# Hedgehog attention and a maxout layer on one core: q and k transposed in blocks of two tokens, q projected by 64-row pairs, its maximum applied as a factor on one of two numerator sums

## The chip, the cores and the metric

The kernel runs on one core of one Trainium2 chip. The metric is the device time of one execution in microseconds (us). The engines are called by their names or by the profile's short ones: TensorE (PE, its weight loads PEld), VectorE (DVE), ScalarE (ACT), GpSimd (POOL), and SyncE (SP), which issues transfers.

## The reference

Inputs q, k, v have 8 batches x 8 heads x 576 tokens x 64; `w_phi` is 64 x 128. The attention result is laid out as 4608 tokens x 512 and goes through a maxout layer of three 512 x 768 matrices and one 768 x 512 matrix.

```python
def phi(x):
    proj = x @ w_phi                                   # 64 -> 128
    proj = proj - max(abs(proj), axis=-1, keepdims=True)
    return concatenate([exp(proj), exp(-proj)], axis=-1)   # as in the reference: the max is subtracted once, then +/-

q_p, k_p = phi(q), phi(k)
kv  = einsum('bhsf,bhsd->bhfd', k_p, v)
z   = sum(k_p, axis=tokens)
num = einsum('bhsf,bhfd->bhsd', q_p, kv)
den = einsum('bhsf,bhf->bhs', q_p, z)[..., None] + 1e-06
x   = num / den                                        # 4608 x 512
h   = maximum(maximum(x @ w1, x @ w2), x @ w3)
out = h @ w_out
```

With m the maximum of |proj| of a token, the first half of the features is exp(proj - m), and the second, exp(-(proj - m)), is exp(-proj + m).

## The kernel before, in words

**Units.** The attention is done in 16 units; a unit is four heads of one batch, taken as two pairs `pr`, each of two heads `ab`. A pair's tokens lie on the partitions (64 per head, two heads above each other) in 9 columns, so a unit has 18 tiles of 128 tokens by 64 features. Units 0 to 3 (`BY_PE`) have q and k transposed by TensorE, units 4 to 15 by a transposing transfer on SP's queue. Unit 0 loads q and k on SP in float32 and casts them on VectorE and ScalarE, units 1 to 3 load them with a casting transfer on POOL's queue, units 4 to 15 load float32 and cast on POOL (line 474).

**Steps of a unit, by the node kinds of the code.**
- `T`, `Tc`: the transposition and its copy to `qkT`. Before, `qkT` holds q on partitions 0 to 63 and k on 64 to 127 of the same 128 columns.
- `G` (line 531): projections with the tokens as outputs, 64 rows each, q and k as a pair on the two row halves; five groups of 4, 4, 4, 4 and 2 tiles, each into two PSUM banks, `psq` and `psk`. ScalarE writes exp(+/-proj) of k to `Ek` (line 544), VectorE takes the maxima of |proj| of q and k (line 550) into `mqp` and `mk`.
- `R`, `mT`, `V` (units 2 to 15): the maxima of q are transposed by TensorE (line 558), copied to SBUF (line 562) and written by a transfer (line 566) into row 64 of `qkT`, in the place of a row of k that is no longer needed.
- `M` (lines 610 to 615): the projection of q with the features as outputs, in five products. The stationary matrix `wphi_m` has -1 in row 64, so the maximum is subtracted by the product itself. In units 0 and 1 it is subtracted by small extra products with `minus` (line 615). ScalarE writes exp(+/-) of it to `Eq` (line 623).
- `E`, `va`, `vd`: exp(-m) and exp(+m) of k (`em`), multiplied into v on POOL (line 585).
- `K` (line 639): 72 products into `kvps`; `kv`: their copies.
- `N` (line 657): ten products for one head of a pair, a numerator *block*; the two halves of the features are added in PSUM, in one bank `psn` of 5 x 65. Four blocks in a unit.
- `x` (lines 663, 664): the reciprocal of column 65 and the quotient, on VectorE.
- `X`: the transposition of the result to `xT`, by TensorE with a copy `Xc` in units 0 and 1, by a transfer on SP after that.

**The maxout layer** runs in nine chunks of 512 tokens: eight of one batch each, once its two units are done, and a last one from the ninth columns of all batches. max(x w1, x w2, x w3) is taken as x w1 plus a maximum of differences: 12 `up` steps of four 512-wide products each (line 710) with the `w_bf` differences (line 781), evictions `t1` on ScalarE or VectorE (lines 718, 720) and `h` on VectorE (line 716), then four `down` steps (lines 738, 743), their copies `osb` (line 751) and stores (line 758).

**What sets the order.** A table written out in the source, `PLAN`, gives every node its engine, its place in the order and its buffers. `plan` sorts the nodes by the table and each engine runs its share in this order; nothing is decided at run time but the waits on semaphores. All PSUM tiles share eight banks, and the table names the bank. `fill` puts products on constants (`idler`) into TensorE's planned gaps.

## Time and profile before

| | |
|---|---|
| time of the kernel, median of 3 runs | 283.17 us (282.54 to 283.33) |
| span of the profiled execution, first to last instruction | 281.1 us |
| what lies around the span, median less span | 2.1 us |
| PE busy | 273.2 us, 97% |
| DVE busy | 201.2 us, 72% |
| ACT busy | 197.0 us, 70% |
| POOL busy | 126.6 us, 45% |

The profile doesn't give a time of its execution besides the span, so the profiled execution's own time is taken as the span and 2.1 us around it. Busy time of TensorE counts a product from its start to its modelled end; neighbouring products overlap, so the distance from one start to the next is the better price. The shares are means over the head, the attention stretch (to about 235 us) and the maxout layer's end, which have different limits; they are to be read by stretch.

### The profile page before, as it was taken

How to read it: one execution, taken by the hardware profiler on the slowest of the kernel's cores; microseconds unless marked ns; L12 is line 12 of the kernel's file. 1: busy time of each engine (PE TensorE's matmuls, PEld its weight loads, DVE VectorE, ACT ScalarE, POOL GpSimd, SP SyncE). 2: the span in 40 equal slices, each digit the busy share in tenths (PEclk: the TensorE clock that was granted, in tenths of full speed). 3: DMA queues.
4: the chain of work that ended last, by engine and by line, in shares of the span. 5: the costliest groups of instructions: out<-in, count | busy, mean ns of one | idle time of the engine just before them, and what ended most of it. 6: DMA issues, size and time to landing. Idle time of an engine off the chain costs nothing.

```text
span 281.1 us, 8518 instructions
## 1 busy us (share of the span) xinstructions
PE 273.2 (97%) x3542; PEld 153.6 (55%) x3542; DVE 201.2 (72%) x426; ACT 197.0 (70%) x455; POOL 126.6 (45%) x112
## 2 busy tenths in 40 slices
PE   8889999999999999998999999999999999999995
PEld 3567665565565565565455556554544655444442
DVE  3999899998799797976798769875565383225342
ACT  3899889997889997876877998787737590321111
POOL 5489999847734634855528481410601500000000
PEclk9999999999999999999999999999999999999999
DMA  7999998999999989799997987976021035331065
GB/s 230 210 212 259 322 215 245 289 269 204 253 204 341 152 158 357 174 264 234 257 232 228 323 187 160 219 152 178 3 47 40 3 77 94 75 77 37 8 141 188
DMA packets 67552, 51.43 MB, mean 183 GB/s; under 512 B 48762, under 2 KB 52922, under 8 KB 67514
## 3 DMA queue, kind: packets, MB, share of 16 engines
q1 hardware_dynamic: 62084, 42.21, 62.1%
q0 software_dynamic: 4720, 7.87, 12.8%
q10 hardware_dynamic: 710, 0.83, 0.8%
q8 instruction: 27, 0.44, 0.6%
q14 instruction: 11, 0.09, 0.1%
HBM read 34.64 MB, written 9.44 MB: 157 GB/s over the span
## 4 chain that ended last, share of the span: by engine, by line
PE 81%; POOL 7%; DMA 6%; DVE 3%; issue 1%; ACT 1%; POOLq 0%
PE ups L710 30%; PE ops L743 15%; PE ops L738 11%; PE psn L657 6%; PE kvps L639 6%; PE psq L531 4%; PE psm L610 4%; DMA q_raw<-in_q_dram 3%; POOL vab L585 2%; DMA qk_bf<-in_k_dram 2%; POOL w_bf L781 2%; POOL qk_bf L474 2%; DVE mqp L550 1%; PE pm L807 1%; DVE mk L550 1%
## 5 line engine op out<-in xcount | busy, mean ns | idle before, releaser
L585 POOL TENSOR_TENSOR vab<-v_raw,em 128x1152 bf16<-128x1152 f32 (+1 forms) x36 | 68.2, 1908 | 83.9 <-ACT em L581 39.5
L710 PE MATMUL ups<-xT,w_bf 128*128 128x512 bf16 x432 | 102.4, 379 | 0.1
L544 ACT ACTIVATE Ek<-psk 128x512 bf16<-128x512 f32 (+1 forms) x156 | 81.5, 575 | 11.9 <-PE psk L531 9.3
L623 ACT ACTIVATE Eq<-psm 128x512 bf16<-128x512 f32 (+1 forms) x160 | 80.4, 584 | 3.5 <-PE psm L610 2.8
L710 PEld LDWEIGHTS <-w_bf 128*128 128x128 bf16 x432 | 40.7, 98 | 45.1 <-DVE x_sb L664 0.2
L550 DVE TENSOR_REDUCE mqp<-psq 128x4 bf16<-128x512 f32 (+1 forms) x80 | 48.5, 632 | 9.8 <-PE psk L531 9.7
L550 DVE TENSOR_REDUCE mk<-psk 128x4 f32<-128x512 f32 (+1 forms) x78 | 48.4, 635 | 4.3 <-PE psk L531 2.3
L743 PE MATMUL ops<-wout_bf,hT 128*128 128x512 bf16 (+2 forms) x222 | 51.1, 373 | 0.0
L716 DVE TENSOR_TENSOR hT<-hT,ups 128x512 bf16<-128x512 bf16 x54 | 35.6, 681 | 19.8 <-PE ups L710 18.7
L751 ACT COPY osb<-ops 128x512 f32<-128x512 f32 x25 | 14.6, 589 | 33.2 <-PE ops L743 24.1
L664 DVE TENSOR_TENSOR x_sb<-psn,rden 128x320 bf16<-128x320 f32 x64 | 31.5, 492 | 2.2
L743 PEld LDWEIGHTS <-hT 128*128 128x128 bf16 x222 | 20.5, 98 | 22.0
L718 ACT ACTIVATE hT<-ups 128x512 bf16<-128x512 f32 x32 | 18.8, 616 | 18.2 <-PE ups L710 18.1
L657 PEld LDWEIGHTS <-Eq 128*128 128x128 bf16 x640 | 25.7, 97 | 9.5 <-issue 0.6
L657 PE MATMUL psn<-kv_sb,Eq 128*128 128x65 bf16 x640 | 27.4, 193 | 0.1
L738 PE MATMUL ops<-xT 128*128 128x512 bf16 x96 | 24.2, 379 | 0.0
L720 DVE TENSOR_SCALAR hT<-ups 128x512 bf16<-128x512 f32 x22 | 15.0, 686 | 12.5 <-PE ups L710 12.5
L531 PE MATMUL psq<-w,qkT 64*128 64x128 bf16 x284 | 23.3, 217 | 0.4 <-DVE qkT L494 0.2
L531 PE MATMUL psk<-w,qkT 64*128 64x128 bf16 x284 | 23.1, 217 | 0.0
L639 PE MATMUL kvps<-vab,Ek 64*128 64x65 bf16 x1152 | 20.6, 190 | 2.5 <-POOL vab L595 1.0
L531 PEld LDWEIGHTS <-qkT 64*128 64x128 bf16 x568 | 16.4, 94 | 10.1 <-issue 7.9
L610 PE MATMUL psm<-qkT,wphi_m 128*128 128x512 bf16 (+1 forms) x70 | 21.8, 358 | 0.0
(78 smaller groups left out, 231.3 us busy)
## 6 DMA issues: line engine op xcount, KB each, us to landing
out_dram<-osb SPq DMA_DIRECT2D x64, 128.0 KB
v_raw<-in_v_dram SPq DMA_DIRECT2D x14, 576.0 KB
k_raw<-in_k_dram SPq DMA_DIRECT2D x11, 576.0 KB
q_raw<-in_q_dram SPq DMA_DIRECT2D x10, 576.0 KB
w_bf<-in_moe_w_dram POOLq DMA_DIRECT2D x3, 768.0 KB, 16.0
v_raw<-in_v_dram POOLq DMA_DIRECT2D x2, 576.0 KB, 13.9
q_raw<-in_q_dram POOLq DMA_DIRECT2D x2, 576.0 KB, 12.1
qk_bf<-in_q_dram POOLq DMA_DIRECT2D x3, 288.0 KB, 9.9
```

The lines of the kernel that those rows point to most:

```text
L531: nc.tensor.matmul(ps()[:, i, :], lhsT=cols[r, :], rhs=w2[r, c, :], start=True, stop=True)
L544: nc.scalar.activation(Ek[s]()[:, tiles_of(t0, n), :], of(1), EXP, scale=1.0 - 2.0 * s)
L550: nc.vector.tensor_reduce((mq, mk)[c]()[:, tiles_of(t0, n)], of(c), AXX, ALU.max, apply_absolute_value=True)
L585: (nc.vector if n_.eng == "DVE" else nc.gpsimd).tensor_tensor(vab()[:, g, t0:t1, 0:D], vb()[:, t0:t1, :], em()[:, g, t0:t1].unsqueeze(2).t ...
L610: nc.tensor.matmul(psm()[:, 0:w], lhsT=wphi_m, rhs=rhs, start=True, stop=True)
L623: nc.scalar.activation(Eqb()[s][:, cols], psm()[:, 0:w], EXP, scale=1.0 - 2.0 * s)
L639: nc.tensor.matmul(kvps[ab]()[:, t // NT, g, :], lhsT=Ek[g]()[r, t, :], rhs=vab()[r, g, t, :], start=(t + g == 0), stop=(t == UT - 1 and g ...
L657: nc.tensor.matmul(psn()[:, c, :], lhsT=Eqb()[g][:, t0:t0 + P], rhs=kv()[:, pr, ab, g, :], start=(g == 0), stop=(g == 1))
L710: nc.tensor.matmul(ups(), lhsT=w_bf[i + 1][:, ct, j * P:(j + 1) * P], rhs=tokens_of(ct), start=(ct == 0), stop=(ct == CT - 1))
L716: nc.vector.tensor_tensor(hT()[:, j, :], hT()[:, j, :], ups(), ALU.max)
L738: nc.tensor.matmul(ops_()[:, 0:width], lhsT=tile_of(ct, tt), rhs=line_w[c_i > MOVE][:, ct, cols], start=(ct == 0), stop=False)
L743: nc.tensor.matmul(ops_()[:, 0:width], lhsT=hT()[:, j, tt * P:(tt + 1) * P], rhs=wout_bf[:, j, cols], start=False, stop=(j == JT - 1))
```

## The change

**Layout.** q and k no longer share columns. `qkT` has a half for q and a half for k, each of nine blocks of 128 columns; a block holds two neighbouring tokens' columns, one on partitions 0 to 63, the other on 64 to 127. A transposition by TensorE is then one 128 x 128 product for two tokens (19 for a unit, where units 1 to 3 had 36 with half the outputs). POOL's cast of q becomes three instructions, since the two ninth columns are put side by side.

**G.** The pair of 64-row products is now two tokens of the same tensor; q and k have groups of their own, each of four blocks into two banks. The ninth columns have a group (`last`) of three pairs: k, q, and the projection of q with features as outputs.

**M.** The maximum of q isn't subtracted any more. Its products are two pairs of 512-wide ones on 64 rows each, with `wphi2` (w_phi on both halves of the partitions) as the stationary matrix. `R`, `mT`, `V`, `minus`, `wphi_m` and the extra products of units 0 and 1 are gone.

**N and x.** exp(proj - m) and exp(-proj + m) are replaced by exp(proj) and exp(-proj); the quotient stays the same if the first sum gets the factor exp(-2m). So the two halves of the features go to two PSUM banks. `cf` (ScalarE, four instructions a unit) makes the factors, `xa` multiplies the first sum by them (VectorE, 5 x 65), `xb` adds the second, `xr` is the reciprocal, and the quotient `x` may run on VectorE or POOL. The eps of the reference is in neither kernel.

**Narrow instructions.** The exponentials of the ninth columns are eight of 128 columns in a unit, where there were four of 256.

**The table.** `PLAN` is new throughout. It puts 21 quotients on VectorE and 43 on POOL, four copies `Tc` on ScalarE, 13 of the evictions `t1` on VectorE where it had 22. Unit 2 comes before unit 1, and the first maxout product stands behind K and three blocks of N of unit 2, where it stood behind unit 1. `gate`, behind which POOL's casting loads stand, waits for the second half of q of unit 0, which SP issued first and now issues third. The last step of the maxout layer is 384 columns wide, where it was 128. The rows of the output go out in another order of tiles, in as many stores of the same size.

The diff, cut to its core (the old loop over `GROUPS` and the table are left out):

```diff
-    wphi_m = const.tile([P, DF], BF16, name="wphi_m")
+    wphi2 = const.tile([P, DF], BF16, name="wphi2")
-    mqp = [const.tile([P, P], BF16, name=f"mqp{i}") for i in range(NE)]
+    mx = [const.tile([P, 2, 2, NT + 1], FP32, name=f"mx{i}") for i in range(NE)]
+    cfs = [const.tile([P, 2, 2, 6], FP32, name=f"cf{i}") for i in range(NE)]
...
-        qkT = un["qkT"] = buf("qkT", 3, [P, UT * P], BF16)
+        qkT = un["qkT"] = buf("qkT", 3, [P, 2, NT * P], BF16)
...
+                            nc.tensor.transpose(tps()[:, n, :], qk()[:, what, t:t + 2, :].rearrange("p t d -> p (t d)"), ident)
...
+        for i in range(2):
+            for what in (1, 0):
+                pss = [bank("psp", [P, 4, DF]) for _ in range(2)]
+                def proj(i=i, what=what, pss=pss):
+                    for n in range(4):
+                        at = (5 * i + n) * P
+                        for par in range(2):
+                            r = slice(par * D, (par + 1) * D)
+                            nc.tensor.matmul(pss[par]()[:, n, :], lhsT=qkT()[r, what, at:at + P], rhs=wphi2[r, :], start=True, stop=True)
...
+            def mm(i=i, pss=pss):
+                for par in range(2):
+                    r = slice(par * D, (par + 1) * D)
+                    rhs = qkT()[r, 0, 5 * i * P:(5 * i + 4) * P].rearrange("p (t ab i) -> p ab t i", ab=2, i=D)
+                    nc.tensor.matmul(pss[par](), lhsT=wphi2[r, :], rhs=rhs, start=True, stop=True)
...
+        def factors():
+            for ab in range(2):
+                for s in range(2):
...
+                    nc.scalar.activation(dst, src, EXP, scale=-2.0)
...
-                psn = bank("psn", [P, 5, W])
+                psn = [bank("psn", [P, 5, W]) for _ in range(2)]
...
+                    for g in range(2):
+                        for c in range(5):
+                            nc.tensor.matmul(psn[g]()[:, c, :], lhsT=Eqb()[g][:, at:at + P], rhs=kv()[:, pr, ab, g, :],
+                                             start=True, stop=True)
...
-                    nc.vector.reciprocal(rden(), psn()[:, :, D:W])
-                    nc.vector.tensor_tensor(x_sb()[:, pr, :, ab, :], psn()[:, :, 0:D], rden().to_broadcast([P, 5, D]),
-                                            ALU.mult)
+                    nc.vector.tensor_tensor(near(), psn[0](), cf()[:, pr, ab, 0:5].unsqueeze(2).to_broadcast([P, 5, W]), ALU.mult)
+                    nc.vector.tensor_tensor(near(), psn[1](), near(), ALU.add)
+                xr = nd("xr", {"DVE": 0.08}, lambda near=near, rden=rden: nc.vector.reciprocal(rden(), near()[:, :, D:W]), [xb],
+                    (nc.vector if n_.eng == "DVE" else nc.gpsimd).tensor_tensor(
+                        x_sb()[:, pr, :, ab, :], near()[:, :, 0:D], rden().to_broadcast([P, 5, D]), ALU.mult)
```

653 lines of the change are left out of this document (322 added, 331 removed).

## The prediction

> **What bounds the kernel now.** I read the table of stretches first, because a share over the whole span mixes the head, the attention stretch and the tail. Its columns are the stretch, its length, then busy time and instructions of PE, PEld, DVE, ACT and POOL, the granted clock, the DMA share and GB/s.
>
> ```profile
> span 281.1 us, 8518 instructions
> ```
>
> ```profile
> 0.00:8.10 8.10, 6.91 (x32) 2.82 (x33) 3.15 (x15) 3.30 (x4) 5.27 (x14) 1.00 0.78 233
> 0.00:39.40 39.40, 36.21 (x645) 23.98 (x645) 32.98 (x79) 31.67 (x76) 31.97 (x40) 1.00 1.06 247
> 39.40:277.80 238.40, 237.02 (x2901) 129.60 (x2897) 167.84 (x347) 165.29 (x380) 94.66 (x73) 1.00 0.72 173
> 39.40:182.00 142.60, 141.24 (x2075) 81.26 (x2072) 121.31 (x255) 123.61 (x290) 82.72 (x64) 1.00 0.97 237
> 42.00:56.00 14.00, 14.00 (x183) 7.58 (x182) 13.11 (x25) 13.69 (x34) 12.63 (x9) 1.00 1.00 266
> ```
>
> The cut at 39.4 is the first product of the maxout layer, and 277.8 is the end of the last product, as the order of time on TensorE shows (start, length, line, tiles, count):
>
> ```profile
> 39.44 1.90 PE L710 MATMUL ups<-xT,w_bf 128*128 128x512 bf16 x8
> ```
>
> ```profile
> 277.28 0.50 PE L743 MATMUL ops<-wout_bf,hT 128*128 128x128 bf16 x6
> ```
>
> From 39.4 to 277.8 TensorE is busy 237.0 of 238.4 us at clock 1.00: it is the bound, and its work there sets the end. Before 39.4 it isn't: its busy time holds filler products. VectorE (33.0) and ScalarE (31.7) do the head's work, and the maxout layer can't begin until units 0 and 1 have gone through both. So the time is the start of the first maxout product, plus TensorE's work behind it, plus what it idles, plus an end of 3.3 (277.8 to 281.1) and 2.1 outside the span: 39.4 + 237.0 + 1.4 + 3.3 + 2.1 = 283.2, which is the median of the runs (283.17); I sum against that.
>
> **What the steps cost.** Prices are distances from one start to the next where instructions stand close. On TensorE:
>
> ```profile
> 82.64 0.22 PE L558 MATMUL pmT<-ident,mqp 128*128 128x128 bf16 x1
> 82.69 1.89 PE L710 MATMUL ups<-xT,w_bf 128*128 128x512 bf16 x8
> 84.42 0.38 PE L610 MATMUL psm<-qkT,wphi_m 128*128 128x512 bf16 x1
> 84.73 0.23 PE L531 MATMUL psq<-w,qkT 64*128 64x128 bf16 x1
> ...
> 85.08 0.22 PE L531 MATMUL psq<-w,qkT 64*128 64x128 bf16 x1
> 85.08 0.22 PE L531 MATMUL psk<-w,qkT 64*128 64x128 bf16 x1
> 85.14 0.22 PE L531 MATMUL psq<-w,qkT 64*128 64x128 bf16 x1
> 85.14 0.22 PE L531 MATMUL psk<-w,qkT 64*128 64x128 bf16 x1
> 85.29 0.39 PE L610 MATMUL psm<-qkT,wphi_m 128*128 128x512 bf16 x1
> ...
> 88.96 1.26 PE L639 MATMUL kvps<-vab,Ek 64*128 64x65 bf16 x72
> 90.06 0.22 PE L531 MATMUL psq<-w,qkT 64*128 64x128 bf16 x1
> ...
> 95.07 0.48 PE L657 MATMUL psn<-kv_sb,Eq 128*128 128x65 bf16 x10
> 95.38 0.27 PE L610 MATMUL psm<-qkT,wphi_m 128*128 128x256 bf16 x1
> ```
>
> A 512-wide product takes 0.216 (eight in 1.73), a 256-wide one half of that, 0.11. The transposition R takes 0.05, K 1.10, a numerator step N 0.31. Two 64-row products on the two row halves start together, and the next pair follows 0.055 behind. A change between 128 rows and 64 rows costs 0.095 each way (84.42 + 0.216 to 84.73; 85.14 + 0.055 to 85.29), 0.19 for an excursion.
>
> **Removed from TensorE.** M, the projection of q for Eq, is four 512-wide and one 256-wide product in a unit, 0.97; it becomes two pairs of 512 and one pair of 128, 0.49. That two halves run together is shown for 128-wide products alone; for 512-wide ones the price of a pair lies between 0.216 and 0.432, and I take 0.216, since the rows' pairs start in the same 10 ns. Thirteen units lie behind the first maxout product in the new table (M of unit 2 has gone ahead) where fourteen did: 13.6 becomes 6.3, 7.3 saved. R: 13 x 0.05 = 0.7. K and three of four N of unit 2 move ahead: 1.1 + 0.9. Four more pairs of G's 64-row products stay behind than before, 0.2 against it. Together 9.8 less. Against it the order has 31 excursions into 64 rows behind that point where it had 25: 1.1 more. So TensorE's work there falls by 8.7, to 228.3.
>
> The two-token transposes, the 18 small products per unit that subtracted the maximum in units 0 and 1, the dropped constant and clears all lie ahead of that point in both tables, where TensorE waits for others: nothing, and if that cover went, a few tenths. The transfer of the maxima (mT, V) leaves SP 12 and ACT's queue 2 issues; it held TensorE up once:
>
> ```profile
> PEld L610 <- DMA qkT<-mT: 0.3, 1, 0.3
> ```
>
> I take nothing for it (0 to 0.3 gained); SP's other issues only move forward.
>
> **Added on VectorE.** Its rows now:
>
> ```profile
> 98.55 0.43 DVE L550 TENSOR_REDUCE mqp<-psq 128x2 bf16<-128x256 f32 x1
> 98.89 0.42 DVE L550 TENSOR_REDUCE mk<-psk 128x2 f32<-128x256 f32 x1
> ...
> 101.02 0.18 DVE L663 RECIPROCAL rden<-psn 128x5 f32<-128x5 f32 x1
> 101.24 0.49 DVE L664 TENSOR_TENSOR x_sb<-psn,rden 128x320 bf16<-128x320 f32 x1
> 101.65 0.68 DVE L550 TENSOR_REDUCE mk<-psk 128x4 f32<-128x512 f32 x1
> 102.24 0.68 DVE L550 TENSOR_REDUCE mqp<-psq 128x4 bf16<-128x512 f32 x1
> ```
>
> A block's end costs 0.63 now (reciprocal 0.22, as the next needs its result, and 0.41). It becomes a scaling xa of 325 numbers (0.415), a sum xb (0.415), the reciprocal xr, and the quotient, which the new table puts on VectorE 21 times (0.41) and on POOL 43 times. xr alone lies between 0.10 (the two reductions, 0.34 and 0.59, give 0.09 fixed and 0.98 ns a column) and 0.22; I take 0.12, as the table mostly puts another instruction between it and its user. So 0.95 a block plus the quotient: 64 x 0.32 + 21 x 0.41 = 29 us more, less 9 maxout evictions of 0.6 that go to ScalarE. The quotient's two inputs both lie in SBUF, which no VectorE row here has: it lies between 0.41, the same form with one input in PSUM, and 0.72, what I get for POOL below; I take 0.41, the same engine's row. The Trainium skill, GPSIMD Engine Reference (Key points), speaks for more: POOL and VectorE share their way into SBUF, and VectorE instructions of two SBUF inputs contend with POOL. By that rule, at 0.72, the four quotients of the head and the five up to unit 5 would put some 1.3 on the time: 283.2. The new wait of xa for the factors is covered: they follow the reductions of q, long before K. Behind a late xa would stand the reductions, and behind those TensorE's banks.
>
> **Added on ScalarE and POOL.**
>
> ```profile
> 108.47 0.33 ACT L581 ACTIVATE em<-mk 128x18 f32<-128x18 f32 x2 [0.41 <-DVE mk L550]
> 108.69 0.36 ACT L644 CAST kv_sb<-kvps 128x260 bf16<-128x260 f32 x1
> 108.95 1.09 ACT L544 ACTIVATE Ek<-psk 128x512 bf16<-128x512 f32 x2
> ```
>
> ```profile
> L585 POOL TENSOR_TENSOR vab<-v_raw,em 128x1152 bf16<-128x1152 f32 x28 | 59.2, 2123 | 79.5 <-issue 38.3 <-ACT em L581 35.1 <-PE ups L710 5.9
> ...
> L585 POOL TENSOR_TENSOR vab<-v_raw,em 128x576 bf16<-128x576 f32 x8 | 9.1, 1152 | 4.4 <-ACT em L581 4.4
> ```
>
> An exponential of 18 columns starts 0.11 behind the one before, one of 512 about 0.49 (1.09 less 0.60, the length of one), so a 128-wide one some 0.19 (bounds 0.11 and 0.49). Four factor instructions cost 0.44 a unit, eight 128-wide ones 1.5. On POOL the two forms give 0.18 fixed and 1.69 ns a column: a quotient 0.72, and two more casts of q 0.37 a unit at most. POOL was busy 82.7 of 142.6 us and has room, except where it also carries the weights' differences.
>
> **The head.** I summed what each table puts ahead of the first maxout product at these prices. For the old one: VectorE 32.7, ScalarE 30.9 (trace: 33.0 and 31.7), so the method holds. For the new one VectorE has 26 full reductions (15.6), 6 half ones (2.0), 18 xa and xb (7.5), 8 xr and 4 quotients (2.6) and 13.1 of copies and casts: 40.8. ScalarE has 56 full exponentials (27.4), 24 narrow ones (4.6) and 9.5 of others: 41.5. The new table starts the maxout layer behind all of units 0, 1 and most of 2. Idle in the first 8.1 us is 4.9 on both and stays; idle up to 39.4 is 6.4 and 7.7. So the first maxout product comes between 46.4 (41.5 + 4.9) and 49.2 (41.5 + 7.7). I take 46.6, near the lower end, as longer queues fill the later idle first: 7.2 later than 39.4. The casting loads of the next units, which now wait for the third load of SP's queue instead of the first, are inside these bounds.
>
> **The cover behind it.** From the first maxout product to the last quotient of unit 13 the new order gives TensorE 150.6 and 29 excursions (5.5), VectorE 147.6, ScalarE 146.2: 95 and 94% of TensorE. Before, over 39.4 to 182, it was 85 and 87%. The row 42 to 56 shows TensorE losing nothing with VectorE at 94 and ScalarE at 98%, so I add no idle; the 1.4 stays.
>
> The sum: 46.6 + 228.3 + 1.4 + 3.3 + 2.1 = 281.7, and 0.2 for the last store, 384 columns wide instead of 128: **281.9**, 1.3 under the median.
>
> **The rivals.** *No change that can be measured* (283.3): the head ends at 48.0, in the middle of its bounds. For it: ScalarE's order has little slack. Against it: its idle behind 8 us was only 2.9.
>
> *Eviction becomes the bound, slower.* Between the first maxout product and the end of unit 5 VectorE has 50.2 and ScalarE 51.3 against TensorE's 49.4 + 2.3. If xr costs 0.22 as the reciprocal does, and xb waits 0.12 for xa's end (0.53 from start to start, if dependent instructions stand a whole length apart as 101.02 and 101.24 do), a block costs 0.22 more, and holds two of the eight banks meanwhile, where it held one. From 0.1 a block VectorE passes TensorE in that stretch (15 blocks, 1.5 us of room); at 0.22 it costs 1.8 there, 0.7 in units 9 to 11, where it has 38.1 against 40.0, and 1.1 in the head, where nine blocks bring VectorE to 42.8 + 4.9 = 47.7: 285.5. The window 42 to 56 speaks against, the thinner margin for it. The Trainium skill, TensorEngine Tiling (Array Packing), Performance Considerations (PSUM Bottleneck), says that packing speeds TensorE up but not the emptying of PSUM; by that rule the saved 8.7 would be lost to VectorE, and no run here shows it.
>
> *The pairs don't run together:* 26 x 0.216 = 5.6: 287.5. The rows at 85.08 and 85.14 speak against.
>
> **Chances.** Forecast 0.50 (280.0 to 282.3), no change 0.25, eviction 0.21, pairs 0.04. A change below 0.3%, 0.85 us, can't be told from none. The range goes from 279.3 (narrow exponentials at 0.11, so that VectorE's 40.8 + 4.9 = 45.7 ends the head, and the idle 1.4 and the wait of 0.3 gone) to 286.9 (eviction's price and the 1.4 of the later head). Faster 0.50, same 0.25, slower 0.25.
>
> **What would show it.** First maxout product near 46.6; TensorE busy about 228 from there to its end, idle under 2; M pairs 0.22 apart; xa to xb not over 0.5 and xr about 0.12; VectorE near 95% up to unit 13. I am wrong if the head ends past 48, or if TensorE's waits name VectorE or ScalarE for several us.

## The result, and the profile after

The changed kernel takes 304.2 us (median of 4 executions, 301.3 to 307.3), the kernel before 283.25 beside it: a ratio of 1.070, 95% interval 1.063 to 1.077. The prediction was 281.9, with a range up to 286.9 and half of its chance on a gain. It is slower by 21 us, more than any rival had. Executions of the changed kernel scatter by 6 us. The slowest shows the lowest mean granted clock (0.954 at 307.3), but the others don't follow that order (0.977 at 303.6, 0.970 at 301.3); the kernel before shows 1.000 in its profile and scatters by 1.4. Ratios and intervals, here and below, are formed without the executions that lie over 1.5% above the fastest of their kernel, and the profiled execution of the changed kernel is one of those left out.

The profiled execution took 307.3, of which 305.4 is its span. Busy times, TensorE and the clock from its page:

```profile
PE 280.9 (92%) x3430; PEld 151.6 (50%) x3430; DVE 238.0 (78%) x498; ACT 215.8 (71%) x590; POOL 160.3 (52%) x171
...
PE   7686789797999999699999999999989999999995
...
PEclk9966959899999999899999999999999999999999
```

The clock row is new: fives and sixes in the first quarter, where the kernel before had nines throughout. The table of stretches, cut as the prediction cut it (columns: stretch, length, busy time and instructions of PE, PEld, DVE, ACT, POOL, granted clock, DMA share, GB/s), and the two rows that give the cuts. The last row of the table is a part of the head at a clock of 0.63:

```profile
0.00:8.10 8.10, 6.03 (x42) 2.50 (x42) 3.70 (x18) 3.09 (x5) 1.97 (x8) 1.00 0.77 251
8.10:58.30 50.20, 39.02 (x596) 24.59 (x591) 39.59 (x82) 40.17 (x115) 37.27 (x37) 0.80 0.99 236
58.30:302.10 243.80, 235.87 (x2798) 124.48 (x2797) 194.75 (x400) 172.15 (x471) 121.08 (x129) 0.99 0.67 152
14.00:28.00 14.00, 9.30 (x139) 6.20 (x139) 8.31 (x15) 8.65 (x30) 8.77 (x12) 0.63 1.18 207
```

```profile
58.33 4.87 PE L739 MATMUL ups<-xT,w_bf 128*128 128x512 bf16 x14
...
300.82 1.14 PE L772 MATMUL ops<-wout_bf,hT 128*128 128x384 bf16 x6
```

The first maxout product comes at 58.3 where 46.6 was predicted (+11.7). From there to the end of the last product it takes 243.6, where 228.3 of work and 1.4 of idle were predicted (+13.9). What follows the last product (3.4) and what lies outside the span (1.9) came out within 0.2 of the prediction. So the 25.4 us between this execution and the prediction lie in two places, and the experiments ask for each.

Three views carry the first reading. POOL in order of time, ahead of unit 0's va (start, length, line, tiles; in brackets the idle time before it and what ended it):

```profile
15.09 0.72 POOL L493 DMA_DIRECT2D qk_bf<-in_k_dram  x1 [0.98 <-DVE mx L550]
18.86 0.72 POOL L453 DMA_DIRECT2D v_raw<-in_v_dram  x1 [3.06 <-DMA w_bf<-in_moe_w_dram]
20.75 0.72 POOL L493 DMA_DIRECT2D qk_bf<-in_q_dram  x1 [1.17 <-DMA qk_bf<-in_q_dram]
21.50 4.47 POOL L638 TENSOR_TENSOR vab<-v_raw,em 128x576 bf16<-128x576 f32 x4
```

The va of unit 0 stand behind three loads more than before, which POOL issues for units 2 and 3, and by this view two of them stop until an earlier load has landed. The trace names the wait: POOL's loads use eight semaphores in turn, and from the ninth on each waits for the landing of the load eight before it, whose semaphore it uses again. So the wait is one of the program, and the twelfth load, at 20.75, waits for the fourth, which landed at 20.46. TensorE waits for va, and K of unit 0 starts at 24.9:

```profile
24.91 0.24 PE L662 MATMUL kvps<-vab,Ek 64*128 64x65 bf16 x2 [3.27 <-POOL vab L638]
```

The tile that holds the quotients (duration least, median, most):

```profile
L697 POOL TENSOR_TENSOR x_sb<-near,rden x43: 717/722/1013, 31.9 to 249.6; 128x320 bf16<-128x320 f32 x43
L697 DVE TENSOR_TENSOR x_sb<-near,rden x21: 477/518/2443, 37.3 to 246.2; 128x320 bf16<-128x320 f32 x21
```

VectorE's quotient takes 0.48 or up to 2.44. And VectorE in order of time, where a scaling (L687) and its sum (L691) stand side by side:

```profile
198.29 0.49 DVE L687 TENSOR_TENSOR near<-psn,cf 128x325 f32<-128x325 f32 x1
198.88 0.50 DVE L691 TENSOR_TENSOR near<-psn,near 128x325 f32<-128x325 f32 x1
199.29 0.68 DVE L745 TENSOR_TENSOR hT<-hT,ups 128x512 bf16<-128x512 bf16 x1
```

From xa to its own xb 0.59, from xb to an instruction that doesn't need it 0.41.

### The profile page after: what moved, and what is told of

It is laid out like the page before. It is cut to its first block, busy times and chain, and to the rows that moved or that the text cites. A ratio compares the mean times of both kernels' runs of the same rounds, so it can differ in the third digit from the quotient of the medians.

```text
span 305.4 us, 8638 instructions
## 1 busy us (share of the span) xinstructions
PE 280.9 (92%) x3430; PEld 151.6 (50%) x3430; DVE 238.0 (78%) x498; ACT 215.8 (71%) x590; POOL 160.3 (52%) x171
## 5 line engine op out<-in xcount | busy, mean ns | idle before, releaser
L550 DVE TENSOR_REDUCE mx<-psp 128x4 f32<-128x512 f32 x128 | 82.5, 678 | 5.6 <-PE psp L563 4.3
L545 ACT ACTIVATE Eq<-psm 128x512 bf16<-128x512 f32 x128 | 72.1, 626 | 7.4 <-PE psm L603 7.2
L539 ACT ACTIVATE Ek<-psp 128x512 bf16<-128x512 f32 x128 | 73.8, 647 | 3.9 <-DVE mx L550 2.9
L697 POOL TENSOR_TENSOR x_sb<-near,rden 128x320 bf16<-128x320 f32 x43 | 32.1, 752 | 34.5 <-DVE rden L693 33.8
L687 DVE TENSOR_TENSOR near<-psn,cf 128x325 f32<-128x325 f32 x64 | 30.5, 486 | 6.7 <-POOL x_sb L697 4.2
L780 ACT COPY osb<-ops 128x512 f32<-128x512 f32 (+2 forms) x26 | 15.4, 592 | 28.1 <-PE ops L772 28.1
L691 DVE TENSOR_TENSOR near<-psn,near 128x325 f32<-128x325 f32 x64 | 30.9, 492 | 3.0
L563 PE MATMUL psp<-wphi,qkT 64*128 64x128 bf16 x512 | 25.6, 223 | 1.8 <-DVE near L687 0.9
L563 PEld LDWEIGHTS <-qkT 64*128 64x128 bf16 x512 | 17.2, 97 | 13.6 <-issue 10.9
L780 DVE COPY osb<-ops 128x512 f32<-128x512 f32 x11 | 7.5, 686 | 20.9 <-PE ops L772 20.9
L662 PEld LDWEIGHTS <-Ek 64*128 64x128 bf16 x1152 | 20.3, 96 | 6.2 <-issue 5.4
```

The costliest lines, as they stand in the source:

```text
L539: lambda: nc.scalar.activation(Ek[s]()[:, ts, :], src(), EXP, scale=1.0 - 2.0 * s), [a], [bank_, Ek[s]],
L545: lambda: nc.scalar.activation(Eqb()[s][:, cols], src(), EXP, scale=1.0 - 2.0 * s), [a], [bank_, Eqb],
L550: lambda: nc.vector.tensor_reduce(dst(), src(), AXX, ALU.max, apply_absolute_value=True), [a, n_const],
L563: nc.tensor.matmul(pss[par]()[:, n, :], lhsT=qkT()[r, what, at:at + P], rhs=wphi2[r, :], start=True, stop=True)
L662: nc.tensor.matmul(kvps[ab]()[:, t // NT, g, :], lhsT=Ek[g]()[r, t, :], rhs=vab()[r, g, t, :], start=(t + g == 0), stop=(t == UT - 1 and g ...
L697: (nc.vector if n_.eng == "DVE" else nc.gpsimd).tensor_tensor(x_sb()[:, pr, :, ab, :], near()[:, :, 0:D], rden().to_broadcast([P, 5, D]), ...
```

## The experiments

"Head" is the start of the first maxout product; "behind" is the time from there to the start of the last product on TensorE; both are from the profiled execution, and the time is the median of all. Waits of TensorE are what the distances between its products have over their price at the granted clock, where that is over 0.15 us, summed behind the head: 1.8 in the kernel before, 11.5 in the profiled execution of the changed one and 11.3 when it ran again, 7.3 with both mends (for which the expectations, by a rougher price, have 8.7).

### Two mends: three loads on POOL, and VectorE's quotient from PSUM

The theories: A, POOL's queue delays the head; B, the quotients on VectorE are slow because POOL works on two SBUF tiles at the same time; C, the clock falls and that costs. The changed kernel ran again beside them.

> The changed kernel unchanged, as the base for the others on the same chip. Theory A (POOL's queue): its casting and float32 loads of units 1 to 4 stand ahead of the products v times exp of unit 0, POOL stops in them between 15.8 and 20.8 us, and K of unit 0 starts near 25 instead of near 20; this is there in every execution. Theory B (quotients): the 21 quotients on VectorE, both inputs in SBUF, take 1.0 us on average instead of 0.41, because POOL's two-input instructions run beside them; there in every execution. Theory C (clock): the lower granted clock from 14 to 70 us is itself the cause, and varies between executions. Expected: 301 to 307 us, quotients on VectorE 0.48 at the least and over 2 at the most, first maxout product near 58.

The loads alone (times of the order's table; the three loads go behind unit 0's four va):

```
-270G0@12.7  190G2@13.4  269G@14.1
+270G0@18.7  190G2@18.8  269G@18.9
```

> Order only: the last three loads on POOL (q and k of unit 3, v of unit 2) stand behind the four products of v and exp of unit 0 instead of ahead of them. Theory A: these products start near 15 instead of 21.5, K of unit 0 near 20, first maxout product 5 to 8 us earlier (50 to 53), time 5 to 8 us less, 295 to 298. Theory B: no change in the head beyond 1 us. Theory C: the clock dips as before, and less than 2 us is gained.

The quotient alone: where VectorE forms it, the sum goes back into its PSUM bank, so that the quotient has one input in PSUM, and xr and x follow the sum at once.

```
-nc.vector.tensor_tensor(near(), psn[1](), near(), ALU.add)
+nc.vector.tensor_tensor((psn[1] if on[0].eng == "DVE" else near)(), psn[1](), near(), ALU.add)
...
-  x_sb()[:, pr, :, ab, :], near()[:, :, 0:D], rden()...
+  x_sb()[:, pr, :, ab, :], (psn[1] if n_.eng == "DVE" else near)()[:, :, 0:D], rden()...
```

> Only the 21 quotients on VectorE change: the sum xb is written back to its PSUM bank, and reciprocal and quotient follow at once and read it there, so that no VectorE instruction has two inputs in SBUF. Theory B: these quotients take 0.48 to 0.50 each (10 us instead of 21 in all), and the time falls by 4 to 10 us, most of it in the stretch from 60 to 250. Theory A: the head stays as it is, and under 2 us is gained. Against both: a block on VectorE now has four instructions that wait for each other, 0.3 us more each, 6 us in all.

> Both edits together. If A and B are two separate causes, the gains add: 9 to 18 us less than the changed kernel, 285 to 294. If the one is only the other's consequence, the sum falls short by the smaller of the two. Theory C alone: no gain, 301 to 307.

| kernel | time | ratio, interval | head | behind |
|---|---|---|---|---|
| changed, again | 301.1 | 1.061 (1.057 to 1.065) | 58.1 | 240.5 |
| loads behind va | 297.2 to 304.1 | none given | 51.5 | 240.0 |
| quotient from PSUM | 301.9 | 1.058 (1.055 to 1.060) | 57.7 | 236.3 |
| both | 295.4 | 1.041 (1.036 to 1.046) | 51.5 | 236.7 |

The four executions with the loads alone took 297.2, 302.6, 304.0 and 304.1.

In the profiled executions the two causes are apart. The loads take 6.5 and 6.2 off the head in the two pairs and little off what is behind it; the quotient takes 4.3 and 3.3 off what is behind it and little off the head. No half-clock stretch lies behind the head in these four, so that part is clear of the clock. In the times neither edit alone shows a gain against 301.1, and both together gain 5.7, where 9 to 18 were forecast for two separate causes. Two limits go with that. The two kernels without the moved loads have two stretches of 6.8 us at half clock in their heads, the two with them one of 3.4, so the loads' share of the head holds what the clock does there. And the edit of the quotient also moves the 21 reciprocals and quotients forward in the table, up to where their sums stand, so its gain behind the head is that of the shorter instruction and of the new order together.

A, in the kernel with the loads moved: POOL now waits for the exponentials, and va starts at 16.4 instead of 21.5.

```profile
16.44 4.47 POOL L638 TENSOR_TENSOR vab<-v_raw,em 128x576 bf16<-128x576 f32 x4 [3.23 <-ACT em L633]
```

B, the group of quotients on VectorE (busy time, mean ns), in the changed kernel run again and in the kernel with both mends:

```profile
L697 DVE TENSOR_TENSOR x_sb<-near,rden 128x320 bf16<-128x320 f32 x21 | 22.0, 1049 | 0.3
```

```profile
L700 DVE TENSOR_TENSOR x_sb<-psn,rden 128x320 bf16<-128x320 f32 x21 | 10.3, 491 | 0.7
```

In the changed kernel's first trace the ten quotients of 0.74 us or more all start inside a two-input POOL instruction of about 2 us (va or the weights' differences), and each ends 0.34 to 0.35 behind that instruction's end. The eleven others meet POOL idle or at its own quotient, or touch such an instruction only at an end, and take 0.48 to 0.52. Two inputs on POOL's side aren't needed: one quotient in the changed kernel run again (1.48 us) and one in the kernel with the loads moved (0.95) ran beside a cast on POOL, which has one input, and ended 0.34 behind the cast's end. With one input in PSUM all 21 take 0.49, eight of them inside a va. The edit takes 11.7 us of VectorE's busy time away and gives 3 to 4, so TensorE didn't wait for each of them. In single times the mends show less than in parts, and the clock goes with these: the kernel with the loads moved took 297.2 at a clock of 0.994 and 304.1 at 0.970.

### The same loads ahead of va in the kernel before

```
-225G0@19.4  226G@21.5  159G2@22.3
+225G0@14.5  226G@14.6  159G2@14.7
```

> The kernel before, with only an order changed on POOL: the same three loads that stand ahead of unit 0's four va in the changed kernel (q and k of unit 3, v of unit 2) go ahead of them here too. Theory A (a load that POOL issues holds everything behind it until earlier loads have landed): unit 0's first va starts near 20 instead of 14.8, unit 0's K near 25 to 26 instead of 20.6, the first maxout product 4 to 6 us later, time 287 to 291, a few us more if the clock falls in the idle time. Rival (the loads are issued while POOL waits for the exponentials anyway): va at most 0.8 later, 283 to 284.

282.9, ratio 0.999 (0.997 to 1.002): the rival's number. But the stop is there:

```profile
12.52 0.72 POOL L457 DMA_DIRECT2D qk_bf<-in_k_dram  x1 [0.66 <-DMA qk_bf<-in_k_dram]
16.31 0.73 POOL L470 DMA_DIRECT2D v_raw<-in_v_dram  x1 [3.07 <-DMA w_bf<-in_moe_w_dram]
17.06 1.17 POOL L585 TENSOR_TENSOR vab<-v_raw,em 128x576 bf16<-128x576 f32 x1
```

The last load stands still for 3.07 us, as in the changed kernel (3.06), yet va starts only 2.2 later than before (14.8), K 0.4, and the head ends 0.2 later. The old order had room between va and K, and its va came at 17.1 and not at 21.5: POOL's first load is issued at 4.4 there and at 7.3 in the changed kernel's first profile, where `gate` waits for the third load of SP's queue; and the last load ahead of va is POOL's eleventh there, which waits for the third to land, and not the twelfth, which waits for the fourth. A is a cause in the new order, not a price of a load as such.

### The clock

The kernel before without its 20 filler products:

```
-        while gap > (0.35 if t < WARM else 0.5) and t < n.start - ...
+        while False and t < n.start - ...
```

> The kernel before without its filler products (20 of them, all before 15.4 us), nothing else changed. Theory C (the granted clock falls when TensorE has been idle, and its price is real): stretches at a clock of 0.5 appear between 10 and 50 us, and the time rises by 2 to 6 us, to 285 to 289, with a scatter between executions. Rival (the head is bound by VectorE and ScalarE, and TensorE's clock there is no matter): clock may fall, time 283 to 284.

287.4, ratio 1.017 (1.009 to 1.025); the head comes at 42.4 instead of 39.4, behind it nothing changes (238.3). Here the clock isn't lost in a dip but comes late: products are long up to 16.8 us, where the kernel before has full clock from 6.4.

```profile
15.13 0.61 PE L612 MATMUL psm<-qkT,w 128*128 128x512 bf16 x1
...
17.79 0.38 PE L612 MATMUL psm<-qkT,w 128*128 128x512 bf16 x1 [0.21 <-DVE mqp L550]
```

So TensorE's clock can have a price in a head that VectorE and ScalarE bound. The next two try to hold it, with 94 fillers instead of 20 (thresholds of `fill` loosened), in the kernel with both mends and in the changed kernel.

> The kernel with both mends, with 94 filler products where it had 20, nearly all ahead of the first maxout product, nothing else changed. Theory C (stretches at half clock follow idle time of TensorE, and an execution pays about 2.6 us for each 0.01 of mean clock, from the executions of the kernel with only the loads moved: 297.2 at 0.994, 302.6 at 0.976, 304.1 at 0.970): the clock stays at 1.00 from 8 us to the end, the time is 290.5 to 293 in every execution, instead of 293.7 to 299.0. Rival (the fillers wait for banks themselves and push the real products back, and the clock had cost little): first maxout product at 53 or later, time 295 to 298.

> The changed kernel as it is, with the same 94 filler products, nothing else changed. Theory C: mean clock rises from 0.954 to 0.977 to 0.98 or more, and the time falls from 301 to 304 to 295 to 299; the hole of 4.4 us ahead of unit 0's K stays, since POOL's queue makes it, so the first maxout product stays at 56 to 58. Rival (the clock is a consequence without a price): 301 to 304.

313.3, ratio 1.109 (1.105 to 1.112), and 312.0, 1.104 (1.099 to 1.109): dearer than any theory had it, and only the first rival's later head came true. 82 of the fillers stand ahead of the first maxout product, which comes at 63.6 in the first and 62.3 in the second.

```profile
0.00:63.60 63.60, 57.37 (x694) 28.40 (x695) 43.06 (x99) 44.04 (x119) 38.65 (x44) 1.00 0.87 218
```

VectorE and ScalarE have little more work there than in the kernel with both mends (43.1 and 44.0 against 41.6 and 42.3), TensorE has 16 us more (57.4 against 41.4). A filler takes TensorE's time and also a bank, which the step that wants the bank may have to wait for; which of the two puts the head back by 12 us, these runs don't tell. What the pair does show: with the clock held (0.989 to 0.995) the four executions of the first lie within 0.3 us, 313.2 to 313.5, against 5 in the kernel with both mends; the second, at 0.995 to 1.000, scatters by 2.6 against 6. The last try takes no bank: each product of G in units 0 to 2 is issued twice into its own.

```
-                    for n in range(4):
+                    for n in [0, 1, 2, 3] * (2 if u < 3 else 1):
```

> The kernel with both mends, in which the 64-row projection products G of units 0 to 2 (8 in a step, 12 steps) are issued twice into the same bank; the second issue writes the same numbers. That adds 12 x 0.22 = 2.6 us of TensorE work to a head where TensorE idles 10 us, and takes no further bank. Theory C (half-clock stretches follow TensorE's idle time and cost about 2.6 us for 0.01 of mean clock): clock 1.00 behind 9 us, every execution at 291.5 to 293.5. Rival (the head has no room for a longer step in a bank, as the 94 fillers showed): the first maxout product 1.5 to 2.6 later than 51.5, time 295 to 297.5 in every execution.

295.5, ratio 1.045 (1.041 to 1.048), no better than 295.4; head 52.1. The head kept its clock, and then a half-clock stretch of 3.4 us came behind it, after waits of TensorE between 114 and 117 us. What a stretch costs where TensorE is the bound can be read from the changed kernel: the 14 products at 58.33 take 4.87 where full clock gives 13 x 0.216 + 0.38 = 3.19, so 1.7 for 3.4 us. Two such stretches lie behind its head (at 58.7 and 126.9), together some 3 us, and the same kernel run again bears that out: it has none there, and 240.5 behind the head instead of 243.3. In the head the profiled execution had three of 6.8, the one run again two, and its first maxout product came only 0.3 earlier. What all of those in the head cost isn't settled, since no kernel held the clock there without lengthening something else.

### Less work for VectorE, less for ScalarE

Two edits, each with something left out of the output: the sum of the two numerators is formed for the denominator's columns alone (and the scaling too, for VectorE's quotients), 29 us less on VectorE; or the factors stay 1, 13.7 us less on ScalarE.

```
-  nc.vector.tensor_tensor((psn[1] ...)(), psn[1](), near(), ALU.add)
+  nc.vector.tensor_tensor((psn[1] ...)()[:, :, D:W], psn[1]()[:, :, D:W], near()[:, :, D:W], ALU.add)
...
-            for ab in range(2):      # factors()
+            for ab in range(0):
```

On the kernel with both mends (295.4) they told nothing, as the clock differed as well: 292.4 to 296.7 at 0.977 to 0.987 with VectorE's work taken away, ratio 1.042 (1.034 to 1.050), and 298.3 at 0.964 to 0.971 without the factors, 1.056 (1.051 to 1.061), above both forecasts.

> The kernel with both mends (three loads behind unit 0's va, VectorE's quotients from PSUM), in which the sum of the two numerators is formed for the denominator's five columns alone, and the scaling too where VectorE forms the quotient (so the second numerator sum is left out of the output). It takes 64 x 0.35 + 21 x 0.35 = 29 us of VectorE work away, what the change had added. Theory B (VectorE's block ends are what TensorE waits for behind the head): TensorE's waits behind the first maxout product, 8.7 us in the kernel with both mends, fall to 2 to 4, and the time from 295.4 to 288 to 291. Rival D (ScalarE's evictions are what TensorE waits for): waits stay above 7, time 293.5 to 296. Both leave the first maxout product at 50 to 51.5, since ScalarE's queue sets the head.

> The kernel with both mends without the four factor instructions of each unit on ScalarE (the factors stay 1, so that the maximum of q is left out of the output). They take 0.21 us each, 0.86 a unit, where the prediction had 0.44. Theory D (ScalarE's queue sets the head and the waits behind it): the first maxout product comes 2 to 2.6 earlier than 51.5 (three units' factors lie ahead of it), waits behind it fall by 1 to 3, time 291 to 293 instead of 295.4. Rival B (VectorE is what it waits for): 51 to 51.5, and 294.5 to 296.

So they were made again where the clock holds better: with 94 fillers (base 313.3), and with G issued twice (base 295.5).

> The kernel with both mends and 94 fillers, in which the second numerator sum is left out but for the denominator's columns, so that VectorE has 29 us less to do. Theory B (VectorE's block ends hold up TensorE behind the head): TensorE's waits behind the first maxout product fall from 7 to 9 us to under 4, and the time is 3 to 6 us under that of the filled kernel with both mends. Rival D (ScalarE does): less than 1.5 under it.

> The kernel with both mends and 94 fillers, without the four factor instructions of each unit (the maximum of q is left out of the output), so that ScalarE has 13.7 us less to do, 2.6 of it ahead of the first maxout product. Theory D (ScalarE's queue sets the head, and its evictions the waits behind it): first maxout product 2 to 2.6 earlier, time 3 to 5 us under that of the filled kernel with both mends. Rival B: less than 1.5 under it.

> As the kernel with both mends and G issued twice in units 0 to 2, with the second numerator sum left out but for the denominator's columns: 29 us less on VectorE. Theory B (VectorE's block ends make the waits behind the head): 4 to 6 us under that kernel, the TensorE waits behind the first maxout product at 6 or less. Rival: under 1.5 us less.

> As the kernel with both mends and G issued twice in units 0 to 2, without the factor instructions (the maximum of q is left out of the output): 13.7 us less on ScalarE, 2.6 of it in the head. Theory B: less than 1.5 us under that kernel, as with 94 fillers (0.8). Rival D (ScalarE's queue sets the head): first maxout product 2 to 2.6 earlier, 3 to 5 us under.

| base | all | VectorE less 29 | ScalarE less 13.7 |
|---|---|---|---|
| 94 fillers | 313.3 | 307.9, ratio 1.088 (1.085 to 1.092) | 312.6, 1.107 (1.101 to 1.113) |
| G twice | 295.5 | 291.6, 1.031 (1.028 to 1.033) | 293.3, 1.038 (1.035 to 1.040) |

In time VectorE's block ends are worth 3.9 to 5.4, the factors 0.8 to 2.3, which is the size that theory B gave and less than D's. The waits, though, don't do what B said, under 4 and 6 or less. They name VectorE less, and others come in their place, as the view of waits shows for the kernel with G twice and less for VectorE (who waits, for whom, idle time in us, times, longest):

```profile
PE kvps L662 <- POOL vab L638: 1.6, 1, 1.6
PE psp L563 <- DMA qkT<-qk_bf: 0.6, 2, 0.3
```

Added up from the distances, the waits of the kernel with G twice are 7.8 us, 3.4 of them for ScalarE and 3.2 for VectorE; with VectorE's work taken away they are 8.2, with 3.9 and 0.5; without the factors 5.7, with 0.0 and 3.8. In the filled kernels they are 9.3, 8.8 and 8.4. The profiled execution with less for VectorE is the slowest of its six, so the place of VectorE's gain isn't shown. D's second half, fewer waits, comes true in the one pair and by 0.9 in the other. Its first half fails: without the factors the first maxout product comes at 53.1 and 52.4 instead of 2 to 2.6 earlier, with half-clock stretches in these heads, and at 63.1 against 63.6 in the filled pair, with none. Both edits together:

> As the kernel with both mends and G issued twice in units 0 to 2, without the factors and with the second numerator sum left out but for the denominator's columns: 29 us less on VectorE and 13.7 us less on ScalarE together. Theory E (each of the two engines alone was nearly full, so taking work from one left the other as the bound): the two gains are more than additive, first maxout product at 48 to 49.5, waits of TensorE behind it under 5, time 284 to 288. Rival (both gains are only what each took from its own queue, 3.9 and 2.3 us, and the rest is the order itself): 288.5 to 290.5, waits of 6 to 8.

289.0 to 290.9, ratio 1.024 (1.020 to 1.028): 5 us off the base, no more than the sum of the two, as the rival said; its waits couldn't be read. (The profiled executions of this kernel and of the first one with VectorE's work taken away took 686 and 934 us, with every TensorE product two to three times as long; why is open, and they are left aside.) So with 43 us of work taken off both evicting engines the kernel still stands 7 us above the kernel before.

### VectorE's added work, alone, in the kernel before

One instruction in the form of xa in each block's end, in its bank, ahead of the reciprocal (numerator and denominator both times 2):

```
+nc.vector.tensor_tensor(psn(), psn(), twos.unsqueeze(2).to_broadcast([P, 5, W]), ALU.mult)
 nc.vector.reciprocal(rden(), psn()[:, :, D:W])
```

> The kernel before with one more VectorE instruction in each block's end, the form of xa: the numerator sum times 2 in its bank, numerator and denominator alike, so the quotient stays. It adds 64 x 0.42 = 27 us to VectorE, what the change adds, and leaves all else as it was. Theory B (the old order's slack on VectorE, 15% of the attention stretch, doesn't cover it): 8 blocks lie ahead of the first maxout product, 3.4 later there; waits of TensorE behind it rise from 2 to 5 or more; time 288 to 293. Rival (covered): 283 to 285.

And one of the same length that no bank waits for, behind the quotient:

```
+nc.vector.tensor_reduce(aside_m, aside, AXX, ALU.max)
```

> The kernel before with one more VectorE instruction behind each quotient, a reduction over 325 numbers of a tile that nothing else uses: about the same 64 x 0.4 us of VectorE as in the kernel that scales the sum in its bank (306.0), but no bank waits for it directly. Theory F (VectorE's time is what is lacking): 298 to 305. Rival G (the longer stay of a numerator sum in its bank is what TensorE waits for): 283 to 288.

306.0, ratio 1.083 (1.079 to 1.087), and 294.1, 1.039 (1.036 to 1.042). The forecast for the first, 293 at most, was far too low; the second lies between its two theories. Three stretches behind the head, of the kernel before, of the one with the instruction aside, and of the one with it in the bank:

```profile
51.00:100.00 49.00, 48.67 (x762) 28.64 (x760) 42.88 (x93) 44.83 (x108) 29.98 (x22) 1.00 1.03 234
100.00:182.00 82.00, 81.02 (x1169) 46.55 (x1167) 67.51 (x143) 67.62 (x157) 41.53 (x36) 1.00 0.96 237
182.00:274.00 92.00, 92.00 (x803) 46.31 (x801) 45.34 (x91) 40.82 (x89) 11.94 (x10) 1.00 0.33 72
```

```profile
51.00:100.00 49.00, 47.49 (x726) 27.32 (x725) 46.23 (x102) 42.69 (x105) 26.06 (x19) 1.00 1.01 244
100.00:182.00 82.00, 80.02 (x1141) 45.27 (x1138) 73.11 (x161) 66.32 (x153) 43.69 (x37) 1.00 0.91 223
182.00:285.00 103.00, 100.97 (x881) 50.70 (x879) 58.80 (x124) 46.84 (x104) 14.48 (x12) 1.00 0.36 78
```

```profile
51.00:100.00 49.00, 45.37 (x691) 25.99 (x690) 45.79 (x97) 40.79 (x98) 24.84 (x18) 1.00 1.01 243
100.00:182.00 82.00, 78.58 (x1055) 43.39 (x1053) 71.70 (x154) 64.58 (x151) 44.98 (x37) 1.00 0.84 213
182.00:297.00 115.00, 109.00 (x1003) 54.92 (x1002) 67.95 (x138) 52.03 (x114) 14.46 (x12) 0.99 0.37 79
```

TensorE idles 1.3 us in all in the first three rows, 5.5 in the next, 13.0 in the last, and busy time hides waits that are shorter than a product: behind the head the three kernels take 238.1, 246.9 and 257.9, the last with one half-clock stretch of 3.4. VectorE is at 87 to 94% of the first two stretches in both; and in the third, at 57 and 59%, TensorE still idles 2.0 and 6.0. In the one aside, 0.40 a block, 25.6 us in all, cost 10.9. In the one in the bank the block's end went from 0.63 to 1.17, since the reciprocal stands 0.53 behind the instruction that it needs:

```profile
102.04 0.51 DVE L665 TENSOR_TENSOR psn<-psn,twos 128x325 f32<-128x325 f32 x1 [0.22 <-PE psn L659]
102.58 0.20 DVE L666 RECIPROCAL rden<-psn 128x5 f32<-128x5 f32 x1
102.81 0.49 DVE L667 TENSOR_TENSOR x_sb<-psn,rden 128x320 bf16<-128x320 f32 x1
103.22 0.49 DVE L665 TENSOR_TENSOR psn<-psn,twos 128x325 f32<-128x325 f32 x1
```

That is 0.54 a block, 34 us, and 23 us of time. The largest waits of TensorE that name the quotient, in the kernel with the instruction in the bank and in the one with it aside:

```profile
PE psk L533 <- DVE x_sb L667: 4.4, 6, 1.0
```

```profile
PE psk L534 <- DVE x_sb L667: 1.4, 3, 0.6
```

By the distances, the waits are 18.9 and 9.7, 17.6 and 8.5 of them for VectorE: in the old order VectorE's added work is what TensorE waits for. Per us added the one in the bank costs 0.67, the one aside 0.43. So VectorE's time is lacking (F), and a longer stay in the bank seems to cost on top (G); that the larger amount of work alone raises the price per us isn't ruled out. In an order not made for it, VectorE's part of the change alone costs as much as the whole change did. The new order is made for it and, by the prediction, has 8.7 us less work on TensorE, and still pays.

## Why the prediction was wrong, point by point

**The cover behind the head** is the step that failed most. The prediction found VectorE and ScalarE at 95 and 94% of TensorE, took the window 42 to 56 as proof that TensorE loses nothing at 94 and 98%, and added no idle. That window is 14 us in which the order happened to fit; with work added to the kernel before, TensorE idled at 87 to 94%, and at 57. With both mends it takes 237.0 from the first maxout product to the end of the last product, against 229.7: 7.3 us more, although the clock was at 1.00 there. The term that failed is the idle time: 1.4 was put, and the waits alone are 7.3, 3.3 for VectorE and 3.3 for ScalarE. The largest in the view of waits:

```profile
51.50:288.60 237.10, 232.71 (x2798) 123.65 (x2797) 188.88 (x400) 171.83 (x471) 119.56 (x129) 1.00 0.68 159
```

```profile
PE ups L743 <- DVE x_sb L700: 1.1, 2, 0.8
PE psm L603 <- DVE x_sb L700: 0.6, 1, 0.6
PE psn L680 <- ACT Eq L545: 0.4, 1, 0.4
```

That the evicting engines' added work is what these waits come from is shown for the kernel before, where VectorE's part of it was added. In the changed kernel it is shown in part: taking 43 us off both engines gave 5 us, and taking VectorE's 29 alone left the waits in the profiled execution as they were. What the order itself does to them stays open.

TensorE's own prices held: two 512-wide products on the two row halves do run together, two in the time of one (second row, with the next product 0.22 behind), G costs what it did, and the changes between 128 and 64 rows, 31 each way as counted, cost 0.09 to 0.10. So the 7.3 saved on M were saved, and then given to waits. The Trainium skill, TensorEngine Tiling (Array Packing), Performance Considerations (PSUM Bottleneck), says that tiling speeds TensorE up and not the emptying of PSUM, which may become the bound; the prediction gave that 0.21. The runs agree as far as the waits name the two engines that empty PSUM.

```profile
163.58 1.89 PE L739 MATMUL ups<-xT,w_bf 128*128 128x512 bf16 x8
165.41 0.39 PE L603 MATMUL psm<-qkT,wphi 64*128 64x512 bf16 x2
165.63 0.57 PE L563 MATMUL psp<-wphi,qkT 64*128 64x128 bf16 x14
```

**The block's end** was priced at distances between instructions that don't depend on each other. xa to xb was to be "not over 0.5"; in the changed kernel's trace it is 0.53 to 0.60 in the 29 places where a sum stands right behind its own scaling, and xr stands 0.49 to 0.53 behind its own sum in 19; elsewhere 0.40 to 0.41. That is the eviction rival's mechanism, and about 7 us of VectorE in all. The four factors stand 0.22 apart and not 0.11, so a unit's cost 0.88 where 0.44 was put, 7 us of ScalarE over the kernel; the narrow exponentials came out at 0.16, under the 0.19.

```profile
181.09 0.86 ACT L619 ACTIVATE cf<-mx 64x12 f32<-64x12 f32 x4
```

**The quotient on VectorE** was put at 0.41 with 0.72 as the other bound, by the nearest row of the same engine; beside POOL's two-input work it was 1.0 on the mean and 2.4 at most, past the upper bound. The row that it was nearest to had its input in PSUM, and that was the difference. The Trainium skill, GPSIMD Engine Reference (Key points), had it: POOL contends with VectorE instructions of two SBUF inputs. The trace agrees, with 0.74 to 2.44 us beside POOL's work and 0.48 without it. The prediction weighed that rule and took the row; the 1.3 that it put on the rule stands against the 3 to 4 that the edit gave behind the head, a part of which may be the order.

**The head**: 11.7 late. POOL's queue, with the half-clock stretches that go with it, makes 6.2 to 6.8 of it. The prediction said that the casting loads of the next units "are inside these bounds"; it looked at when the loads may start, and neither at what stands behind them on POOL nor at the landing that the ninth load and those after it wait for. The other 4.9 are left with both mends:

```profile
0.00:8.10 8.10, 6.20 (x24) 2.19 (x26) 2.71 (x16) 1.85 (x3) 2.58 (x10) 1.00 0.76 243
```

```profile
0.00:51.50 51.50, 41.42 (x632) 24.89 (x633) 41.60 (x99) 42.33 (x119) 37.59 (x43) 0.97 1.07 255
```

ScalarE has 42.3 instead of 41.5, 6.25 of idle in the first 8.1 us instead of 4.9 (the casts of k and q that kept it busy there have gone to VectorE), and 2.9 of idle later, as much as in the kernel before, where I had let longer queues fill it: 0.8 + 1.35 + 2.7 = 4.9. That sum says where ScalarE's time lies and not why; taking its factors away did not bring the head forward, so what binds the last 5 us there stays open. One half-clock stretch of 3.4 us is left in this head, at 32.7, which no term of the sum has.

**The clock** was in no step. It stood at 1.00 in every row of before, and the prediction never asked what would happen to it once TensorE waits for 2 to 4 us at a time. The Trainium skill, TensorE: Matmul & The Clock Gate, Part 1: The HAM clock gate, puts the clock at half after an idle window of about 3.4 us. The trace agrees in the length, with half-clock stretches of 3.4 and 6.8 us and products of 0.61 instead of 0.38. It doesn't show that TensorE must be idle so long: its longest wait in the changed kernel's profile is 3.27 us, and yet there are five stretches. In the 3.4 us ahead of the one at 126.9 it was busy for 1.58:

```profile
123.50:126.90 3.40, 1.58 (x20) 0.72 (x19) 1.40 (x4) 1.09 (x2) 3.40 (x4) 1.00 1.09 380
```

Ahead of the other four it was 0.5 to 2.0.

What held: the prices on TensorE, xa, xb and xr where nothing depends on them (0.41, 0.41, 0.10), the quotient on POOL (0.72), the end, the store. "I am wrong if the head ends past 48, or if TensorE's waits name VectorE or ScalarE for several us" named both failures, and the chance for them, 0.25 for anything slower, was too small.

For the 25.4 us of the profiled execution: 6.8 POOL's queue and 4.9 the rest of the head; behind it 3 to 4 the slow quotients and their places in the order, about 3 two half-clock stretches, and some 7 that are mostly waits that name VectorE and ScalarE. The first and the third are shown by taking them away, in profiled executions; the clock's share behind the head by a second execution without it. The last is shown for the kernel before and only in part for the changed one; the rest of the head, and the clock's share in it, are open.

## What to carry to other kernels

When a change moves work from the engine that binds to engines that stand at 85%, price the added work as a loss until a whole stretch, and not one window, shows cover: here 26 and 34 us added to an engine at 85% cost 11 and 23. Price a chain of dependent instructions by the distance between dependent ones, and an operand by where it lies. For each step that is reordered, read what stands behind it on its queue, and look at where TensorE will idle, since that also takes its clock.

## What the hardware showed that was not expected

- A VectorE instruction with two SBUF inputs, started inside a POOL instruction of 2 us, ended 0.34 to 0.35 behind that one's end, in ten of ten cases of one trace: 2.44 us instead of 0.48 at most. Beside a one-input cast on POOL it was the same (1.48 and 0.95). With one input in PSUM it took 0.49 beside the same POOL instructions.
- POOL's eleventh load stood still for 3.06 and 3.07 us in two kernels until the third had landed, whose semaphore it used again, and held POOL's arithmetic behind it.
- On VectorE a dependent instruction followed 0.53 (sum to reciprocal, in SBUF or PSUM) and 0.59 (scaling to sum) behind, an independent one 0.41; on ScalarE four small exponentials stood 0.22 apart, where two others had stood 0.11.
- The clock changed in steps to half and back, in stretches of 3.4 us or multiples of it, also after 3.4 us in which TensorE was busy nearly half of the time; and 62 fillers more ahead of the first maxout product cost more (12 us of head) than the clock that they held.
